# Mixture-of-experts stage: where three pieces of side work are issued (joint-list products on GpSimd, one weight quarter, the third expert's factor copies)

## The chip, the cores and the metric

One core of a Trainium2 chip runs the whole program. A core has five engines, each of which takes its instructions strictly in its own order: TensorE (PE, matmuls; PEld its weight loads), VectorE (DVE), ScalarE (ACT), GpSimd (POOL) and SyncE (SP, which only issues DMAs here). The metric is the device time in microseconds (us) of one execution, the median of the runs; lower is better.

## The reference

Three layers follow each other: a retention layer with a decaying state (input for all that follows: x, 3072 tokens of 512), a soft mixture of experts with 8 experts of 4 slots each, and a sparse mixture of 8 experts of which every token uses the two best.

```python
# last layer; x is (3072, 512), w1 (8, 512, 1024), w2 (8, 1024, 512)
noisy_logits = x @ w_gate + log1p(exp(x @ w_noise)) * noise
top2 = two largest of noisy_logits per token
top2_w = softmax over those two
for e in range(8):
    for k in range(2):
        mask = top2[:, k] == e
        h = maximum(x[mask] @ w1[e], 0)
        out[mask] += top2_w[mask, k, None] * (h @ w2[e])
```

The layer before makes x as c @ slot_out with only 32 slots: every row of x is a mixture of the same 32 vectors, with the weights c.

## The kernel before

The last layer uses that form. With x = c @ slot_out, x @ w1[e] is c @ (slot_out @ w1[e]), so an expert's first weight matrix V1[e] is first multiplied with the 32 slot vectors (g_dot) into a small factor; its split into a high and a low part (g_split) is laid out over the partitions as the factor tile gs, for expert 0 by matmuls (g_rep), for the others by 16 SyncE DMAs of 32 KB (g_copy, L741). Experts are numbered from 0 here, so the third one is expert 2.

Every expert's tokens are gathered as blocks: six full ones of 128 tokens and one of 64 (number 6). Which tokens a block holds is computed on the chip as lists. For experts 0 and 1 there is a list each (lists): a comparison on VectorE (bm, L754), two products on GpSimd (bt, L757 and L758), more comparisons (oh, L761), 24 small matmuls (pli, L765), and two VectorE instructions that give the indices. The lists of the other six experts are made together (lists_all), in two rounds that run during expert 0's blocks and expert 1's first ones: VectorE comparisons bm, rk and oh, two GpSimd products sb (L804), two VectorE products bta of bm and sb (L807), 24 matmuls (L812). lists_all is a generator; it is moved on by one step at the end of the blocks in PACED, (expert, block) = (0, 1) to (0, 5) and (1, 0), and its matmuls are issued at HOOK (0, 4, 4) and (1, 1, 2), that is before step 4 of block 4 of expert 0 and step 2 of block 1 of expert 1.

Of a block, GpSimd gathers the rows of c (fetch, L851) by an indirect DMA, ScalarE and VectorE split them (turn, L863 to L865), TensorE transposes them (L870), multiplies them with the factor tile (hidden, L904; evicted by L907 on ScalarE and L909 and L912 on VectorE), and then with the second matrix V2[e] in 24 matmuls (main, L937 to L939; the small block L941 and L943). V2 is used as a high and a low part too: split_hi is a cast on ScalarE (wh, L879), split_lo a subtraction on VectorE (wl, L885). ScalarE writes the block's result yo (L946), and GpSimd scatters it with an addition into the output (add_rows, L918). Blocks are taken in the order 0, 1, 2, 3, 6, 4, 5 in expert 0 and 0, 6, 1, 2, 3, 4, 5 in the others.

Weights of the coming experts are loaded in quarters of 512 KB, which SyncE issues (L958): V2[e + 1] and V1[e + 3]. The instructions' order on each engine is made when the program is built: an instruction can be placed as soon as what it depends on is there, with the order of the code as priority, however far ahead of its place in the code that is. To tie something to a block's end, a one-element copy on ScalarE reads yo and writes into the tile that the later instruction will fill; these copies are called marks (L777 in lists_all, L957 for the weight quarters). V1[2] is an exception: three of its quarters are loaded after routing (L698), and the last one (L995) after a one-element GpSimd copy (L994) that stands behind the fetches of expert 0. After that quarter, g_rest (HOOK (0, 0, 6)) finishes the product of V1[2] and issues the 16 copies of expert 2's factor tile. The fills (L144) are matmuls without a use.

Of the kernel before, what the change touches and what calls it, by code (L numbers as in the profile page):

```python
# [26 lines left out]
KD = DM // P  # L27
# [78 lines left out]
def kernel(ctx: ExitStack, tc: tile.TileContext, q, k, v, phi, w1, w2,  # L106
                              wg, wn, noise, v1, v2, csta, cst, cst16, out):
    nc = tc.nc
# [24 lines left out]
    def after(*ins):  # L133
        stack = ExitStack()
        for i in ins:
            stack.enter_context(tc.issue_after(i.ins if hasattr(i, "ins") else i))
        return stack
# [22 lines left out]
    def col16(name):  # L160
        o, n = CONST_COLS[name]
        return ct16[:, o:o + n]
# [16 lines left out]
    W1, W2, V1, V2 = {}, {}, {}, {}  # L179
# [30 lines left out]
    with ExitStack() as actx:  # L210
# [284 lines left out]
        wsl = late.tile([P, NCH, E], F32, name="wsl")  # L495
# [50 lines left out]
    with rctx, bctx:  # L546
# [146 lines left out]
        V1[2] = ringp.tile([P, 4096], F32, name="w", tag="w")  # L693
        v1p = v1[2].rearrange("(k p) n -> p k n", p=P)
        with after(put):
            nc.scalar.copy(V1[2].rearrange("p (k n) -> p k n", k=KD)[0:1, :KD - 1, 0:1], wsl[0:1, :KD - 1, 0:1])
        for i in range(KD - 1):
            nc.sync.dma_start(V1[2][:, 1024 * i:1024 * i + 1024], v1p[:, i])  # L698


# [15 lines left out]
    def g_split(pg, n):  # L716
        gr = cc.tile([P, 2, n, QF], F32R, name=f"gr{n}", bufs=1)
        pv = pg[:, :n * QF].rearrange("p (n f) -> p n f", n=n)
        nc.scalar.copy(gr[:, 0], pv)
        nc.vector.tensor_tensor(gr[:, 1], pv, gr[:, 0], op=OP.subtract)  # L720
        return gr

    def g_tile(e):
        gs = cc.tile([P, 4, QF], F32R, name="gs", bufs=4)
        GS[e] = gs.rearrange("p h (k f) -> p (h k) f", f=P)
        return gs

    def g_rep(e, gr, n):
        gs = g_tile(e)
        for g in range(4):  # L730
            gw = psC.tile([P, QF], F32, name="gw", tag="phc", bufs=4)
            for i in range(2):
                nc.tensor.matmul(gw, pselr[32 * g:32 * g + 32, i, :], gr[32 * g:32 * g + 32, i, n],
                                 start=(i == 0), stop=(i == 1))
            nc.scalar.copy(gs[:, g], gw)

    def g_copy(e, gr, n):
        gs = g_tile(e)
        for q in range(4):
            for g in range(4):  # L740
                nc.sync.dma_start(gs[32 * q:32 * q + 32, g].bitcast(F32), gr[32 * g:32 * g + 32, q // 2, n].bitcast(F32))  # L741
# [32 lines left out]
    def lists_all():  # L774

        def mark(ap, y):
            nc.scalar.copy(ap, y[0:1, 0:1])  # L777

        rv = rr.rearrange("p (e c) -> p c e", e=E)
        bv = blk.rearrange("p (c e) -> p c e", e=E)  # L780
        y = yield
        bm = cc.tile([P, NCH, E, LB], F16, name="bma", bufs=1)
        mark(bm[0:1, 0, 0, 0:1], y)
        nc.vector.tensor_tensor(bm, bv[:, :, :, None].to_broadcast([P, NCH, E, LB]),
                                col16("iotab")[:, None, None, :LB].to_broadcast([P, NCH, E, LB]), op=OP.is_equal)
        for i in range(2):
            rk = cc.tile([P, NCH, E], F16, name="rk", bufs=1)
            mark(rk[0:1, 0, 0:1], y)
            nc.vector.tensor_tensor(rk, sels[i], rv, op=OP.mult)
            rs = cc.tile([P, NCH], F32, name="rs", bufs=1)  # L790
            nc.vector.reduce_sum(rs, rk, axis=AX.X)
            rh = cc.tile([P, NCH], F16, name="rh", bufs=1)
            nc.vector.tensor_copy(rh, rs)
            y = yield
            oh = cc.tile([P, NCH // 8, P, 8], F16, name="oh", bufs=1)
            for c in range(NCH // 8):
                mark(oh[0:1, c, 0, 0:1], y)
                nc.vector.tensor_tensor(oh[:, c], tab, rh[:, None, 8 * c:8 * c + 8].to_broadcast([P, P, 8]),
                                        op=OP.is_equal)
            y = yield  # L800
            bt = cc.tile([P, NCH, 2, E, LB], F16, name="bta", bufs=1)
            sb = cc.tile([P, 2, NCH, E], F16, name="sb", bufs=1)
            for a, name in enumerate(("base", "tok")):
                nc.gpsimd.tensor_tensor(sb[:, a], sels[i], col16(name)[:, :, None].to_broadcast([P, NCH, E]),  # L804
                                        op=OP.mult)
                mark(bt[0:1, 0, a, 0, 0:1], y)
                nc.vector.tensor_tensor(bt[:, :, a], bm, sb[:, a, :, :, None].to_broadcast([P, NCH, E, LB]), op=OP.mult)  # L807
            yield
            if i == 0:
                pl = psC.tile([P, 2, E, LB], F32, name="pli", tag="pt")  # L810
            for c in range(NCH):
                nc.tensor.matmul(pl.rearrange("p a e b -> p (a e b)"), oh[:, c // 8, :, c % 8],  # L812
                                 bt[:, c].rearrange("p a e b -> p (a e b)"),
                                 start=(i == 0 and c == 0), stop=(i == 1 and c == NCH - 1))
            if i == 0:
                y = yield
        lt = cc.tile([P, E, LB], F32, name="lta", bufs=1)
        nc.vector.tensor_scalar_add(lt, pl[:, 0], float(N))
        ls = cc.tile([P, E, LB], I32, name="lsa", bufs=1)
        nc.vector.tensor_tensor(ls, lt, pl[:, 1], op=OP.add)  # L820
        for e in range(2, E):
            LS[e] = ls[:, e]
        for g in range(G):
            fetch(2, g)
        yield
# [17 lines left out]
    CG, HOOK = {}, {}  # L843

    def fetch(e, g):
        bs = grp(e, g)
        cg = CG[e, g] = cc.tile([P, 3, NS + E], F32, name="cg", bufs=5)
        if SB in bs:
            nc.gpsimd.memset(cg[TL:, 2, :], 0.0)
        for i, b in enumerate(bs):  # L850
            nc.gpsimd.indirect_dma_start(out=cg[:rows(b), i, :], out_offset=None, in_=ctab,  # L851
                                         in_offset=index(e, b, rows(b)))
            WT[e, b] = cg[:rows(b), i, NS + e:NS + e + 1]
# [127 lines left out]
    with after(his[3], *lists(0, cc, psC, LB)):  # L981
        gr0 = g_split(pgs, 2)
        g_rep(0, gr0, 0)
        pg2 = psC.tile([P, QF], F32, name="pg", tag="phc", bufs=4)
        g_dot(2, pg2, range(KD - 1))
        fill(psC, "pyc", FA)
        fetch(0, 0)
        cg0 = CG[0, 0]
        ga = turn(0, 0)
        fill(psC, "pyc", FT)  # L990
        with after(*ga):
            for g in range(1, G):
                fetch(0, g)
            nc.gpsimd.tensor_copy(V1[2][0:1, 3072:3073], cg0[0:1, 0, 0:1])  # L994
            nc.sync.dma_start(V1[2][:, 3072:], v1p[:, 3])  # L995
        for i in range(4):
            if i > 1:
                split_hi(0, i)
            split_lo(0, i)
        h0, relu = hidden(0, 0)  # L1000
        with after(relu[RL]):
            turn(0, 1)
        HOOK[0, TZ[0], TZ[1]] = (turn, 0, G - 1)
        with after(h0, *ga):
            g_copy(1, gr0, 1)
            lists(1, cc, psC, LB)
            gen = lists_all()
            next(gen)
            for b in PACED:
                PACE[b] = gen.send  # L1010
            HOOK[0, 4, 4] = HOOK[1, 1, 2] = next, gen
    def g_rest():
        g_dot(2, pg2, [KD - 1])
        g_copy(2, g_split(pg2, 1), 0)

    HOOK[0, 0, 6] = g_rest,
    for e in range(E):
        pre = {g: [] for g in range(G)}
        if e + 1 < E:
            pre[0] += [(fetch, e + 1, g) for g in range(G)] if e != 1 else []  # L1020
            for g, at_b in enumerate(TURN):
                HOOK[e, at_b[0], at_b[1]] = (turn, e + 1, g, [] if e else LAST)
            if e >= 2:
                pre[0] += [(g_one, e + 1)]
            pre[0] += [(load_paced, V2, v2, e + 1, e, (0, SB, 1, 2) if e else (0, 1, 2, 3))]
            if e + 3 < E:
                pre[0] += [(load_paced, V1, v1, e + 3, e, (3, 3, 4, 4))]
            pre[G - 1] += [(split_w, e + 1)]
        for g in range(G):
            for f, *a in pre[g]:  # L1030
                f(*a)
            if g + 1 < G:
                last, relu = hidden(e, g + 1)
                LAST[:] = last, relu[-1]
            elif e + 1 < E:
                hidden(e + 1, 0)
            main(e, g)
# [81 lines left out]
```

## Time and profile before

| | |
|---|---|
| median of 3 runs | 589.7 us (586.41, 589.7, 592.46) |
| profiled execution | 592.0 us, of which the span is 590.2 us |
| TensorE busy | 554.7 us, 94% of the span |
| VectorE, ScalarE, GpSimd busy | 255.3, 243.7, 222.5 us |
| mean granted TensorE clock | 0.964 |

The span is the time from the first to the last instruction of one execution that the hardware profiler recorded; the profiled time holds the little that lies around it. Busy shares are averages over stages: routing ends near 212 us, expert 0's first block starts near 225 us, and its last block ends near 279 us. The granted clock is the share of TensorE's full speed (2.4 GHz) that it was allowed; 0.50 is its lower level, 1.2 GHz.

### The profile page before, as it was taken

What the parts mean: (1) busy time and instruction counts of PE and PEld (TensorE: products, weight loads), DVE (VectorE), ACT (ScalarE), POOL (GpSimd) and SP (SyncE); (2) the same over time, 40 slices, a digit from 0 to 9 for tenths busy, and PEclk for the clock granted to TensorE, in tenths of its full rate; (3) what the DMA queues carried; (4) which work ended last, traced back from release to release, by engine and by line L of the source; (5) the groups of instructions that cost most, each with busy time, mean ns of one, the idle gap of its engine ahead of it and who ended that gap; (6) DMA issues with size and microseconds to landing.
All of it is one profiled execution on the core that took longest, in us unless ns stands there. A gap on an engine that the chain in (4) does not pass through costs nothing. (4 is left out here: it accounts for less than half of the span.)

```text
span 590.2 us, 10723 instructions
## 1 busy us (share of the span) xinstructions
PE 554.7 (94%) x4196; PEld 421.8 (71%) x4196; DVE 255.3 (43%) x529; ACT 243.7 (41%) x543; POOL 222.5 (38%) x214
## 2 busy tenths in 40 slices
PE   7999999999899878979999999999999999999990
PEld 4787888787443436858787787787787787788880
DVE  3566777764202366456625235235235234334200
ACT  2555656553101235245246246246345335335210
POOL 3524534330103055642455444344344436332231
PEclk7899999999699789989999999999999999999997
DMA  9999999998799942465446646656656644553232
GB/s 218 286 270 306 299 328 281 308 405 364 291 404 389 367 124 67 102 179 151 108 98 182 125 132 186 124 151 168 137 140 170 143 112 65 132 105 46 37 43 31
DMA packets 79485, 111.76 MB, mean 189 GB/s; under 512 B 10066, under 2 KB 51602, under 8 KB 78530
## 3 DMA queue, kind: packets, MB, share of 16 engines
q1 hardware_dynamic: 65808, 95.96, 49.3%
q0 software_dynamic: 9696, 14.37, 16.7%
q10 hardware_dynamic: 3922, 0.66, 0.6%
q8 instruction: 35, 0.57, 0.4%
q14 instruction: 24, 0.20, 0.1%
HBM read 87.92 MB, written 20.41 MB: 184 GB/s over the span
## 5 line engine op out<-in xcount | busy, mean ns | idle before, releaser
L937 PE MATMUL pyc<-wh,hhl 128*128 128x512 f32 x384 | 154.6, 403 | 0.2 <-ACT hhl L907 0.2
L938 PE MATMUL pyc<-wl,hhl 128*128 128x512 f32 x384 | 152.1, 396 | 0.0
L939 PE MATMUL pyc<-wh,hhl 128*128 128x512 f32 x384 | 151.5, 395 | 0.0
L918 POOL DMA_INDIRECT out_dram<-yo,lsa x42 | 66.1, 1575 | 136.1 <-ACT w L957 31.6
L909 DVE SCALAR_TENSOR_TENSOR hhl<-phc,hhl 128x512 fp32r<-128x512 f32 (+1 forms) x128 | 66.9, 551 | 84.9 <-ACT hhl L907 84.5
L939 PEld LDWEIGHTS pyc<-wh,hhl 128*128 128x128 f32 x384 | 72.6, 189 | 16.6
L937 PEld LDWEIGHTS pyc<-wh,hhl 128*128 128x128 f32 x384 | 72.1, 188 | 16.1 <-ACT hhl L907 0.4
L946 ACT ACTIVATE yo<-pyc,cg 128x512 f32<-128x512 f32 x48 | 33.0, 688 | 121.0 <-PE pyc L939 108.1
L938 PEld LDWEIGHTS pyc<-wl,hhl 128*128 128x128 f32 x384 | 72.4, 189 | 14.6
L907 ACT ACTIVATE hhl<-phc 128x512 fp32r<-128x512 f32 (+1 forms) x128 | 59.5, 513 | 8.0 <-PE phc L904 6.6
L885 DVE TENSOR_TENSOR wl<-w,wh 128x1024 fp32r<-128x1024 f32 x32 | 39.1, 1225 | 49.6 <-ACT wh L879 49.6
L851 POOL DMA_INDIRECT cg<-ctab,lsa x42 | 43.8, 1042 | 15.2 <-issue 14.9
L879 ACT CAST wh<-w 128x1024 fp32r<-128x1024 f32 x32 | 33.4, 1047 | 32.3 <-DMA w<-in_moe_w_dram 24.7
L298 DVE TENSOR_TENSOR am<-pa,cta 128x512 f32<-128x512 f32 x48 | 33.1, 692 | 28.6 <-PE py L322 15.3
L918 POOL DMA_INDIRECT out_dram<-yo,ls x14 | 25.0, 1787 | 47.4 <-ACT w L957 16.2
L256 POOL TENSOR_TENSOR comp<-raws,cta 64x512 f32<-64x512 f32 x24 | 24.9, 1039 | 40.7 <-PE py L322 16.5
L276 DVE TENSOR_TENSOR qT<-pt,cta 64x512 f32<-64x512 f32 x48 | 33.0, 688 | 16.6 <-PE pt L271 16.2
L256 POOL TENSOR_TENSOR vl<-raws,cta 64x512 f32<-64x512 f32 x24 | 24.9, 1038 | 33.5 <-PE py L322 22.6
L904 PE MATMUL phc<-cts,gs 128*128 128x256 f32 (+1 forms) x192 | 36.5, 299 | 0.5 <-ACT cts L873 0.5
L904 PEld LDWEIGHTS phc<-cts,gs 128*128 128x128 f32 x192 | 29.8, 191 | 7.3 <-issue 2.5
L294 PE MATMUL pa<-qT,kT 64*128 64x128 f32 x384 | 31.7, 296 | 0.7 <-DVE qT L276 0.7
L294 PEld LDWEIGHTS pa<-qT,kT 64*128 64x128 f32 x384 | 27.0, 198 | 5.2 <-issue 3.7
(195 smaller groups left out, 701.6 us busy)
## 6 DMA issues: line engine op xcount, KB each, us to landing
w<-in_moe_w_dram SPq DMA_DIRECT2D x80, 512.0 KB, 5.1
w<-in_moe_w_dram SPq DMA_DIRECT2D x11, 2048.0 KB, 10.5
comp<-in_q_dram SPq DMA_DIRECT2D x12, 512.0 KB, 6.7
out_dram<-zt SPq DMA_DIRECT2D x6, 1024.0 KB, 9.8
raws<-in_k_dram SPq DMA_DIRECT2D x11, 512.0 KB, 5.6
raws<-in_v_dram SPq DMA_DIRECT2D x11, 512.0 KB, 7.8
gs<-gr SPq DMA_DIRECT2D x112, 32.0 KB, 2.3
w<-in_moe_w_dram SPq DMA_DIRECT2D x2, 1024.0 KB, 21.1
```

The costliest lines, as they stand in the source:

```text
L256: pool_ins[0] = nc.gpsimd.tensor_tensor(VL[j][rs], RAW[u][1][gs, :, r, :], gv[gs, r, t, :, None].to_broadcast([64, H, D]), op=OP.mult)
L294: mm = nc.tensor.matmul(pa[s][:, hp, :], KT[j][r, hp, :], QT[t][r, hp, g, :], start=True, stop=True)
L851: nc.gpsimd.indirect_dma_start(out=cg[:rows(b), i, :], out_offset=None, in_=ctab, in_offset=index(e, b, rows(b)))
L879: ins = nc.scalar.copy(wh, V2[e][:, 1024 * i:1024 * i + 1024])
L885: nc.vector.tensor_tensor(wl, V2[e][:, 1024 * i:1024 * i + 1024], WH[e][i], op=OP.subtract)
L904: nc.tensor.matmul(ph[:, w * i:w * i + w], GS[e][:, kf + i], CT[e, g][:, :w], start=True, stop=True)
L907: relu.append(nc.scalar.activation(h[:, :, :w], pv, AF.Relu))
L909: last = nc.vector.scalar_tensor_tensor(h[:, :, w + t0:w + t0 + 2 * P], pv[:, :, :2 * P], 0.0, h[:, :, :2 * P], op0=OP.max, op1=OP.subtract)
L918: nc.gpsimd.indirect_dma_start(out=out, out_offset=index(e, b, n), in_=y, in_offset=None, bounds_check=N - 1, oob_is_err=False, compute_op ...
L937: nc.tensor.matmul(py, hhl[:, kf, ts], wh, start=(kf == 0), stop=False)
L938: nc.tensor.matmul(py, hhl[:, kf, ts], wl, start=False, stop=False)
L939: nc.tensor.matmul(py, hhl[:, kf, tl], wh, start=False, stop=(kf == KF - 1))
```

## The change

Three edits. In lists_all, a mark on the product tile sb is put ahead of each of the two GpSimd products, so that they wait for the block's result, as the VectorE products behind them did already. The last quarter of V1[2] is loaded by the same loop as the other three, and its own GpSimd copy and load behind the fetches are gone. The copies of expert 2's factor tile are taken out of g_rest, which now keeps only the split, and are issued at HOOK (0, 3, 5), before step 5 of block 3 of expert 0.

```diff
         with after(put):
-            nc.scalar.copy(V1[2].rearrange("p (k n) -> p k n", k=KD)[0:1, :KD - 1, 0:1], wsl[0:1, :KD - 1, 0:1])
-        for i in range(KD - 1):
+            nc.scalar.copy(V1[2].rearrange("p (k n) -> p k n", k=KD)[0:1, :, 0:1], wsl[0:1, :KD, 0:1])
+        for i in range(KD):
             nc.sync.dma_start(V1[2][:, 1024 * i:1024 * i + 1024], v1p[:, i])
...
             for a, name in enumerate(("base", "tok")):
+                mark(sb[0:1, a, 0, 0:1], y)
                 nc.gpsimd.tensor_tensor(sb[:, a], sels[i], col16(name)[:, :, None].to_broadcast([P, NCH, E]),
                                         op=OP.mult)
...
         fetch(0, 0)
-        cg0 = CG[0, 0]
         ga = turn(0, 0)
         fill(psC, "pyc", FT)
         with after(*ga):
             for g in range(1, G):
                 fetch(0, g)
-            nc.gpsimd.tensor_copy(V1[2][0:1, 3072:3073], cg0[0:1, 0, 0:1])
-            nc.sync.dma_start(V1[2][:, 3072:], v1p[:, 3])
...
     def g_rest():
         g_dot(2, pg2, [KD - 1])
-        g_copy(2, g_split(pg2, 1), 0)
-
+        gr2.append(g_split(pg2, 1))
+
+    gr2 = []
     HOOK[0, 0, 6] = g_rest,
+    HOOK[0, 3, 5] = (lambda: g_copy(2, gr2[0], 0)),
```

## Rows read from the trace of the kernel before

**Rows 1.** Busy time by stretch: bounds, length, busy per engine, granted clock, DMA share, GB/s

```profile
211.92:215.37 3.45, 0.00 (x1) 0.14 (x1) 2.65 (x4) 3.45 (x6) 3.29 (x4) 1.00 0.98 351
254.04:257.75 3.71, 0.00 (x0) 0.03 (x1) 3.71 (x8) 1.56 (x9) 2.31 (x1) 1.00 0.46 114
257.82:261.24 3.42, 3.42 (x11) 2.79 (x12) 0.16 (x1) 1.63 (x7) 0.00 (x0) 0.50 0.59 103
262.00:582.00 320.00, 314.91 (x1599) 250.54 (x1597) 119.20 (x246) 133.50 (x300) 130.80 (x103) 1.00 0.54 123
```

**Rows 2.** Timeline, VectorE, GpSimd, TensorE: start, length, instruction, count, idle before and releaser

```profile
211.81 0.33 DVE L754 TENSOR_TENSOR bm<-blk,ct 128x168 f16<-128x168 f16 x1
212.03 1.98 POOL L804 TENSOR_TENSOR sb<-sel,ct 128x192 f16<-128x192 f16 x2 [3.36 <-PE pg L185]
213.98 0.92 POOL L757 TENSOR_TENSOR bt<-bm,ct 128x168 f16<-128x168 f16 x1
214.86 0.47 POOL L758 TENSOR_TENSOR bt<-bm,ct 128x168 f16<-128x168 f16 x1
215.37 1.57 PE L765 MATMUL pli<-bt,oh 128*128 128x14 f16 x24 [3.45 <-POOL bt L758]
```

**Rows 3.** Timeline, GpSimd, first gather of expert 0

```profile
217.63 1.91 POOL L851 DMA_INDIRECT cg<-ctab,ls  x1 [2.31 <-DVE ls L770]
```

**Rows 4.** Timeline, SyncE's queue, 209 to 262 us

```profile
210.51 1.30 SPq L698 DMA_DIRECT2D w<-in_moe_w_dram  x3
215.68 2.53 SPq L741 DMA_DIRECT2D gs<-gr  x3
227.79 0.34 SPq L995 DMA_DIRECT2D w<-in_moe_w_dram  x1
228.18 18.97 SPq L741 DMA_DIRECT2D gs<-gr  x29
247.25 14.96 SPq L958 DMA_DIRECT2D w<-in_moe_w_dram  x5
```

**Rows 5.** Timeline, ScalarE and TensorE, expert 0's blocks 0 to 3

```profile
237.81 0.19 ACT L957 COPY w<-yo 1x1 f32<-1x1 f32 x1
242.19 0.69 ACT L946 ACTIVATE yo<-pyc,cg 128x512 f32<-128x512 f32 x1 [4.18 <-PE pyc L939]
252.43 1.05 ACT L879 CAST wh<-w 128x1024 fp32r<-128x1024 f32 x1 [4.06 <-DMA w<-in_moe_w_dram]
257.75 0.67 PE L870 MATMUL ptc<-identr,st 128*128 128x128 f32 x3 [3.72 <-DVE st L865]
```

**Rows 6.** One line's instructions: the weight quarters of L958, 262 to 330 us

```profile
DMA to landing us min/median/max: 3.4/4.0/6.3
```

**Rows 7.** Timeline, joint lists, first round (block 3 of expert 0)

```profile
261.42 3.02 DVE L807 TENSOR_TENSOR bta<-bma,sb 128x1344 f16<-128x1344 f16 x2
261.60 2.81 POOL L918 DMA_INDIRECT out_dram<-yo,ls  x1 [4.62 <-ACT w L957]
264.66 0.97 POOL L804 TENSOR_TENSOR sb<-sel,ct 128x192 f16<-128x192 f16 x2
268.31 1.68 PE L812 MATMUL pli<-bta,oh 128*128 128x112 f16 x24
```

**Rows 8.** Timeline, joint lists, second round (block 0 of expert 1)

```profile
281.08 1.56 POOL L918 DMA_INDIRECT out_dram<-yo,ls  x1 [4.95 <-ACT hhl L907]
286.25 3.03 DVE L807 TENSOR_TENSOR bta<-bma,sb 128x1344 f16<-128x1344 f16 x2 [2.04 <-ACT bta L777]
290.09 1.68 PE L812 MATMUL pli<-bta,oh 128*128 128x112 f16 x24
```

**Rows 9.** Timeline, TensorE, first matmuls of expert 1's list

```profile
230.34 0.61 PE L765 MATMUL pli<-bt,oh 128*128 128x14 f16 x8 [0.85 <-POOL bt L758]
```

**Rows 10.** Scatters of L918, 236 to 300 us: landing; and the waits of the whole run

```profile
DMA to landing us min/median/max: 2.5/5.4/8.2
...
POOL out_dram L918 <- DMA out_dram<-yo,lsa: 26.7, 10, 5.2
```

## The prediction

> **What bounds the kernel now.** Read the busy time by stretch first [rows 1]: from 262 to 582 us TensorE works 314.91 of 320.00 us at full clock. There a change gains nothing, and a microsecond saved or lost ahead of it moves the end by a microsecond. What can be saved lies where TensorE stands still: the same view has two holes between routing and the second expert, 211.92 to 215.37 and 254.04 to 257.75, and behind the second one 3.42 us at a granted clock of 0.50, that is 1.2 instead of 2.4 GHz, in which TensorE is busy throughout.
>
> Then ask of each hole what ended last. The first ends when GpSimd has the second of the two products of expert 0's list [rows 2]: the list's matmul L765 waited 3.45 us for L758. The products could have begun at 212.14, when VectorE had their operand (L754), but GpSimd was then making two products of the joint lists (L804, 1.98 us), which stand in the code behind expert 0's fourth block. They had no operand that is late, so the build's scheduling placed them there, in front of the products that TensorE waits for.
>
> The second hole ends with VectorE's L865 [rows 5], but VectorE had been held up itself. In the rows of ScalarE the cast L879 of expert 1's first quarter of V2 stands idle 4.06 us for its DMA, and the block results and evictions behind it in ScalarE's order stand with it. Why the quarter came late is read on SyncE's queue [rows 4]: it is issued at 247.25, directly behind 29 copies of the factor tile (18.97 us, 0.65 us each), though the mark that releases it was done at 238.00 (L957, 237.81 and 0.19) [rows 5]. Half of the 32 copies are those of expert 2. And the copies started late because the queue sat behind V1[2]'s last quarter (L995), which was issued at 227.79 after a GpSimd copy that comes behind the fetches.
>
> **Part by part.** The sum is made against the profiled execution: 592.0 us, of which the span is 590.2. It is the slow end of the three runs of before (586.41 to 592.46); their median is 2.3 below it, and I carry the difference over to the median unchanged. One per cent is 5.9 us, as much as these three runs differ among themselves, so it is about what a measurement of this kernel can tell from no change.
>
> 1. *The joint products leave the list of expert 0.* L757 starts when L754 is done, at 212.2 in place of 213.98 [rows 2]. Its length and that of L758 may change, since VectorE's comparisons now run beside both: 1.34 us for the pair as it stands, up to twice 0.92 if both are as slow as L757 was. They end at 213.5 to 214.05 against 215.32, a gain of 1.3 to 1.8; I take 1.4, nearer to the slower end, because the comparisons still run then. All of it lies on the path: list, gather L851 at 217.63 (it waited 2.31 us for the list) [rows 3], then the first block. **Minus 1.4.**
>
> 2. *V1[2]'s fourth quarter with the others.* One more SyncE issue of 0.43 us (1.30 for three) at 211.8, with nothing behind it in that queue until 215.68 [rows 4]. Its 512 KB take 1.5 us more at the 351 GB/s of that stretch [rows 1], so the transfer may still run when the gather, now at 216.2, begins. If the gather had to stand behind all of it, that is 0 to 1.5 us on the path; I take 0, since GpSimd spends 1.91 us on that gather first [rows 3]. Removed are a one-element GpSimd copy (hidden beside gathers) and SyncE's stop from 218.2 to 227.79. The 13 copies of expert 1's tile that now stand behind that stop run on at 218.2 and are done near 227.
>
> 3. *Expert 2's copies later.* The 16 copies (16 x 0.65 = 10.5 us of SyncE) depend on nothing but a split done before block 0 ends, so they may be placed anywhere from there on; but the weight quarters of blocks 0 to 2 now stand ahead of them in the code, and a quarter whose mark is done goes first. So the first quarter of V2[1] is issued at 238.05 in place of 247.25 (behind a few copies, 0.65 each, if they are placed first). Who waits for the copies: expert 2's hidden layer, a whole expert later. Who waits behind them on SyncE: the other quarters of V2[1], whose casts come after expert 0's last block, and V1[3], needed two experts later. Nothing for either.
>
> With the quarter there, the cast L879 doesn't stand idle where it stood, results and evictions run 4 us earlier, and L865 is done before TensorE asks for it: the hole of 3.71 goes, and with it the half clock behind it, which followed on that idle time: 3.42 us of busy work at 0.50 is 1.71 at full clock [rows 1]. **Minus 5.4.** It is 0 if the quarter stays where it was.
>
> What is late next: the same cast. If it is placed in ScalarE's order as soon as its data are expected, it stands ahead of block 1's result, L946 at 242.19 [rows 5]. A quarter lands 4.0 us after issue in the median of the later ones [rows 6], and this one took 5.2 (247.25 to 252.43), with a second quarter right behind it. So landing is between 242.05 and 243.25, the cast takes 1.05, and block 1's result and the evictions behind it come 0.9 to 2.1 us late, or 0 if the cast is placed behind them. One quarter is now alone, so I take a value near the lower end. **Plus 1.2.**
>
> 4. *The joint products held.* ScalarE gets four marks of under 0.2 us each, nothing to it. GpSimd gets a place in line: each product pair now comes behind the block's scatter L918, and VectorE's L807 waits for it. Block 3 first [rows 7]: L807 started at 261.42 and the scatter at 261.60. A scatter alone takes 1.56 us (281.08, [rows 8]), beside L807 it took 2.81. Now 261.60 + 1.56 + 0.3 between instructions + 0.5 (half of L804's 0.97) gives 264.0: L807 comes 2.6 us later and ends near 267.1, against L812's need at 268.31. So the list itself is in time. The evictions of expert 1's hidden layer, if they stay behind L807 in VectorE's order, would be late by up to 2.6; but they are ready sooner than L807 now and will most likely go ahead of it. Between 0 and 2.6 I take 0.
>
> Block 0 of expert 1 is tighter [rows 8]: L807 ran from 286.25 to 289.28, and L812 needs it at 290.09. With the scatter 0.2 behind L807's old start, as in block 3: 286.4 + 1.56 + 0.3 + 0.5 = 288.8, plus 3.03, is 291.8: 1.7 us late if L812 keeps its place among the matmuls, 0 if it is moved back by as much. The nearest row is expert 1's own list, the same sequence of VectorE, GpSimd and TensorE inside running blocks: there TensorE stood 0.85 us [rows 9]. **Plus 0.9.**
>
> One rule speaks against this part. The two L804 took 1.98 us beside VectorE's comparisons and 0.97 without them [rows 2, 7], and the comparisons went on meanwhile: both were slowed, neither seems stopped. The Trainium skill, page "SBUF — State Buffer", section "Who interferes with whom", says that a VectorE instruction with two SBUF inputs and a GpSimd instruction that reads SBUF exclude each other, and that the later one stands until the other is done. By that rule L807 would also wait out the second product, 0.5 more, and the sum would be 4.2 in place of 4.7.
>
> **The sum:** -1.4 - 5.4 + 1.2 + 0.9 = -4.7 us. 592.0 becomes 587.3; on the median, 585.0.
>
> **Rivals.**
> - *No new wait bites.* Cast and L812 are placed behind what would have stood for them. For it: TensorE has other matmuls to take first; against it: both places are within 2 us of their data in the rows. -1.4 - 5.4 = -6.8: 582.9. Chance 0.22.
> - *The holding costs all it can.* VectorE keeps its order and evictions wait 2.6, L812 keeps its place, 1.7: -6.8 + 1.2 + 2.6 + 1.7 = -1.3: 588.4. For it speaks that GpSimd and VectorE take their work strictly in order. Chance 0.15.
> - *The change doesn't do what it says.* Copies wait for nothing late, so the build may place them ahead of the quarter as it placed L804 ahead of the list, and hole two stays: -1.4 + 0.9 = -0.5: 589.2. Chance 0.10.
> - *Slower: held products behind a scatter that must wait for the one before it.* Later in the trace ten scatters stood 26.7 us in all for an earlier one's landing, which comes 2.5 to 8.2 us after issue, 5.4 in the median [rows 10]. The scatter ahead of block (1, 0) is issued at 281.08; from a landing later than 286.4 on, 5.3 us, the products and L812 move with it. At 8.2 they come 2.9 later still: L812 4.6 late, an idle time as long as the ones that the half clock followed, 1.7 more: 6.3. With block 3's 2.6: -1.4 - 5.4 + 1.2 + 2.6 + 6.3 = +3.3: 593.0. Against it: the landing must be at its worst. Chance 0.08.
>
> **How the numbers follow.** The forecast has 0.45. Its own range is 582.5 to 587.5 by the bounds of terms 1 to 4. The range for 8 in 10 takes in the full gain and the costly holding, with the spread of the runs: 581.5 to 590.0. Faster by over 1% is below 583.8: most of the full gain and the lower edge of the forecast, 0.27. Slower by over 1%, above 595.6, needs the last rival and more: 0.04. The rest is 0.69.
>
> **What would show it.** L757 right behind L754, L765 near 214. SyncE issuing a V2[1] quarter about 10 us earlier, before most of expert 2's copies; no hole of 3 us before L870 and no half clock behind it. The cast L879 ahead of or behind block 1's L946 tells the 1.2. L804 directly behind the scatters of blocks (0, 3) and (1, 0), and a TensorE wait before the second L812. It is wrong if that quarter is still issued behind all copies, if hole two has another releaser that is as late, or if L812 stands for several microseconds.

## The result: slower, and the profile after

The changed kernel takes **595.16 us** (588.96 to 599.89, 15 runs) against 589.7 for the kernel before beside it (15 runs); the ratio is 1.0086, with a 95% interval of 1.0056 to 1.0115. A second series of the same kernel gave 592.47 against 591.38, 1.0029 (0.9997 to 1.0061). So the change costs some 1 to 5.5 us; 585.0 was forecast. The profiled execution of the first series took 595.16 us, its span is 593.3. From line 804 of the kernel before on, the changed kernel's lines stand one further down (L805, L808, L813, L919 for L804, L807, L812, L918).

First what was meant to happen. Expert 0's list, timeline of the changed kernel by engine, against [rows 2]:

```profile
205.71 0.32 DVE L754 TENSOR_TENSOR bm<-blk,ct 128x168 f16<-128x168 f16 x1
206.10 0.86 POOL L757 TENSOR_TENSOR bt<-bm,ct 128x168 f16<-128x168 f16 x1 [3.34 <-DVE bm L754]
206.92 0.91 POOL L758 TENSOR_TENSOR bt<-bm,ct 128x168 f16<-128x168 f16 x1
207.88 1.57 PE L765 MATMUL pli<-bt,oh 128*128 128x14 f16 x24 [2.08 <-POOL bt L758]
```

No joint product stands ahead of L757 any more. From L754's start to TensorE's list it is 2.17 us in place of 3.56: 1.4 less.

SyncE's queue, against [rows 4]:

```profile
204.61 1.77 SPq L698 DMA_DIRECT2D w<-in_moe_w_dram  x4
209.57 18.76 SPq L741 DMA_DIRECT2D gs<-gr  x26
236.01 0.39 SPq L959 DMA_DIRECT2D w<-in_moe_w_dram  x1
236.44 3.68 SPq L741 DMA_DIRECT2D gs<-gr  x6
```

The first quarter of V2[1] goes out at 236.01, with no stop ahead of the copies. That is 11.2 us earlier by the trace's clock, but this whole execution runs early; counted from L754 it goes out after 30.3 us in place of 35.4, 5.1 earlier. ScalarE's cast of it is done at 241.6, long before the third block, and TensorE's transposes wait for nothing: hole two [rows 5] is gone. TensorE's timeline of the changed kernel:

```profile
252.14 0.46 PE L871 MATMUL ptc<-identr,st 128*128 128x128 f32 x3
```

Now what was not meant. Timeline of the changed kernel at block (0, 3), by engine:

```profile
255.17 0.19 ACT L777 CAST bta<-yo 1x1 f16<-1x1 f32 x1
...
256.68 1.56 POOL L919 DMA_INDIRECT out_dram<-yo,ls  x1 [3.98 <-ACT hhl L908]
257.68 1.55 POOL L805 TENSOR_TENSOR sb<-sel,ct 128x192 f16<-128x192 f16 x2
...
258.81 3.32 DVE L808 TENSOR_TENSOR bta<-bma,sb 128x1344 f16<-128x1344 f16 x2 [3.21 <-POOL sb L805]
262.05 0.41 DVE L910 SCALAR_TENSOR_TENSOR hhl<-phc,hhl 128x256 fp32r<-128x256 f32 x1
262.39 0.21 DVE L913 SCALAR_TENSOR_TENSOR hhl<-phc,hhl 128x64 fp32r<-128x64 f32 x1
...
262.74 0.60 PE L905 MATMUL phc<-cts,gs 128*128 128x320 f32 x1 [3.17 <-DVE hhl L913]
```

Read it downwards. The marks are done at 255.36. The block's scatter goes first, and starts only 1.3 us later; the products come behind it; VectorE, which has L808 as the next instruction in its order, stands 3.21 us until 258.81. Its two L808 then take 3.32 us, the evictions of the next hidden layer come behind them, and TensorE waits 3.17 us for those. At block (1, 0) the same sequence ends in the list itself:

```profile
286.30 1.56 POOL L919 DMA_INDIRECT out_dram<-yo,ls  x1 [3.80 <-ACT w L958]
287.93 0.97 POOL L805 TENSOR_TENSOR sb<-sel,ct 128x192 f16<-128x192 f16 x2
...
288.47 3.31 DVE L808 TENSOR_TENSOR bta<-bma,sb 128x1344 f16<-128x1344 f16 x2 [5.00 <-POOL sb L805]
...
291.83 1.38 PE L813 MATMUL pli<-bta,oh 128*128 128x112 f16 x18 [2.29 <-DVE bta L808]
```

And each stand is followed by half clock. Busy time by stretch of the changed kernel, columns as in [rows 1] (the two holes, and what follows each):

```profile
259.57:262.74 3.17, 0.00 (x1) 0.03 (x1) 3.17 (x5) 0.00 (x0) 0.00 (x0) 0.89 0.97 280
262.03:268.85 6.82, 6.11 (x32) 5.03 (x33) 4.72 (x18) 2.12 (x6) 0.82 (x1) 0.50 0.14 26
289.54:291.83 2.29, 0.00 (x1) 0.00 (x0) 2.29 (x3) 1.04 (x1) 0.00 (x0) 1.00 0.50 86
292.75:296.16 3.41, 3.41 (x18) 2.92 (x17) 1.61 (x4) 0.19 (x1) 2.68 (x2) 0.50 0.44 150
```

Where the time went is easiest seen from the starts of the block results (L946, after the change L947). The table takes, from each kernel's timeline: the end of expert 0's list (L770) and the start of the first block's main product, both from the start of L754; then the time from that main product to the result of block (0, 3), from there to that of (0, 4), from the result of (1, 0) to that of (1, 1); last the result of block (1, 4), again from L754. What lies ahead of L754 differs from execution to execution (205.7 to 213.8 us) and is left out by this. The names are those of the experiments below.

```
kernel                      list  main   to 0,3  to 0,4  1,0 to 1,1  (1,4)
before                      5.5   13.4   34.8    12.9    10.9        103.9
after                       4.2   17.5   30.8    18.2    14.7        113.1
e9  after, again            4.2   14.8   30.8    18.2    14.9        110.6
e1  hold alone              4.2   13.2   33.9    17.4    13.2        109.5
e2  quarter alone           5.4   13.8   30.4    12.3    10.9         99.2
e3  copies alone            6.0   13.8   32.5    12.3    10.9        101.4
e4  quarter + copies        5.8   14.8   29.3    12.4    10.9         99.2
e5  e4 + first held         4.2   13.8   29.9    17.0    10.9        103.5
e6  e4 + second held        5.9   14.8   29.4    12.3    15.5        103.9
e7  e4 + held early         4.2   14.0   29.7    12.3    10.8         99.3
e8  after, products first   4.2   15.2   28.9    12.8    10.9         99.7
e10 e2 + held early         4.2   15.1   28.6    12.3    10.9         98.8
e11 held early alone        4.2   12.2   33.9    13.8    10.9        102.6
```

The changed kernel gains 4.0 us up to block (0, 3) and loses 5.3 and 3.8 at the two held blocks. In its first profile it also loses 4.1 ahead of the first main product, which is looked at in e9.

### The profile page after: what moved, and what is told of

Same layout as the page of the kernel before. It is cut to its first block, busy times and chain, and to the rows that moved or that the text cites. A ratio compares the mean times of both kernels' runs of the same rounds, so it can differ in the third digit from the quotient of the medians.

```text
span 593.3 us, 10733 instructions
## 1 busy us (share of the span) xinstructions
PE 552.6 (93%) x4196; PEld 421.4 (71%) x4196; DVE 255.4 (43%) x529; ACT 242.9 (41%) x547; POOL 217.1 (37%) x213
## 5 line engine op out<-in xcount | busy, mean ns | idle before, releaser
L939 PE MATMUL pyc<-wl,hhl 128*128 128x512 f32 x384 | 153.8, 401 | 0.0
L919 POOL DMA_INDIRECT out_dram<-yo,lsa x42 | 65.8, 1566 | 132.0 <-ACT yo L947 32.6
L940 PEld LDWEIGHTS pyc<-wh,hhl 128*128 128x128 f32 x384 | 73.5, 191 | 17.1
L938 PEld LDWEIGHTS pyc<-wh,hhl 128*128 128x128 f32 x384 | 73.3, 191 | 15.7
L939 PEld LDWEIGHTS pyc<-wl,hhl 128*128 128x128 f32 x384 | 73.4, 191 | 15.2
L947 ACT ACTIVATE yo<-pyc,cg 128x512 f32<-128x512 f32 x48 | 33.0, 688 | 119.6 <-PE pyc L940 110.6
L852 POOL DMA_INDIRECT cg<-ctab,lsa x42 | 40.9, 974 | 26.4 <-issue 23.5
L905 PE MATMUL phc<-cts,gs 128*128 128x256 f32 (+1 forms) x192 | 37.7, 306 | 8.1 <-DVE hhl L913 3.2
L919 POOL DMA_INDIRECT out_dram<-yo,ls x14 | 24.2, 1725 | 47.3 <-ACT hhl L908 17.5
L905 PEld LDWEIGHTS phc<-cts,gs 128*128 128x128 f32 x192 | 30.4, 196 | 15.6 <-issue 8.8
L294 PE MATMUL pa<-qT,kT 64*128 64x128 f32 x384 | 30.0, 286 | 1.3 <-DVE qT L276 1.3
L294 PEld LDWEIGHTS pa<-qT,kT 64*128 64x128 f32 x384 | 25.2, 188 | 5.8 <-issue 3.7
```

The costliest lines, as they stand in the source:

```text
L294: mm = nc.tensor.matmul(pa[s][:, hp, :], KT[j][r, hp, :], QT[t][r, hp, g, :], start=True, stop=True)
L905: nc.tensor.matmul(ph[:, w * i:w * i + w], GS[e][:, kf + i], CT[e, g][:, :w], start=True, stop=True)
L919: nc.gpsimd.indirect_dma_start(out=out, out_offset=index(e, b, n), in_=y, in_offset=None, bounds_check=N - 1, oob_is_err=False, compute_op ...
L938: nc.tensor.matmul(py, hhl[:, kf, ts], wh, start=(kf == 0), stop=False)
L939: nc.tensor.matmul(py, hhl[:, kf, ts], wl, start=False, stop=False)
L940: nc.tensor.matmul(py, hhl[:, kf, tl], wh, start=False, stop=(kf == KF - 1))
```

## The experiments

My theory after the result was that the holding costs 5 to 8 us and the quarter 3 to 5, and that the copies gain about 4. The first four kernels take the change apart, beside 589.44 us for the kernel before.

**e1, hold alone** (the kernel before with one line more):

```
             for a, name in enumerate(("base", "tok")):
+                mark(sb[0:1, a, 0, 0:1], y)
```

> The kernel before with the marks on the joint products alone. My theory from the two traces: the list of expert 0 ends 1.4 us earlier, but in blocks (0, 3) and (1, 0) the products stand behind the scatter, VectorE waits for them with the evictions behind, and TensorE stands about 3.2 us and 2.3 us, each followed by some half clock worth 1.7 to 2: in all 5 to 8 us more than before. The rival, that the holding costs nearly nothing and the loss is elsewhere, expects 1.4 us less to 1 us more.

597.1 us, ratio 1.0101 (1.0060 to 1.0142). **e2, quarter alone:**

```
...
-        for i in range(KD - 1):
+        for i in range(KD):
             nc.sync.dma_start(V1[2][:, 1024 * i:1024 * i + 1024], v1p[:, i])
...
-            nc.gpsimd.tensor_copy(V1[2][0:1, 3072:3073], cg0[0:1, 0, 0:1])
-            nc.sync.dma_start(V1[2][:, 3072:], v1p[:, 3])
```

> The kernel before with the fourth quarter of V1[2] loaded with the others, alone. My theory: the rest of that product and its split on ScalarE are now placed ahead of the first evictions of expert 0, and the first block starts about 4 us later: 3 to 5 us more than before, with a TensorE hole and half clock between 216 and 228 us. The rival, that those stops in the trace of after were an accident of one execution, expects no change, 1 us less to 1 us more. Both expect the hole before L870 near 254 us to stay, since the 32 copies still stand ahead of the first quarter of V2[1].

584.08 us, ratio 0.9887 (0.9852 to 0.9923); one of its six runs took 2969.87 us and is not in the ratio. **e3, copies alone:**

```
-        g_copy(2, g_split(pg2, 1), 0)
+        gr2.append(g_split(pg2, 1))
...
+    HOOK[0, 3, 5] = (lambda: g_copy(2, gr2[0], 0)),
```

> The kernel before with expert 2's copies issued later, alone. My theory: the first quarter of V2[1] is issued some 10 us earlier, the hole before L870 and its half clock go (-5.4 us), and the cast that is now ahead of block 1's result costs 0.7 to 1.4: about 4 us less than before, 3 to 5. The rival, that the wait only moves to the cast ahead of block 1's result and what it saves is lost there, expects no change within 1 us.

587.29 us, ratio 0.9955 (0.9929 to 0.9982). **e4, quarter and copies** (the changed kernel without the two marks):

> The changed kernel without the marks on the joint products: quarter and copies together. My theory: +4 from the quarter and -4 from the copies, so as before within 1.5 us. The rival, by which the quarter costs nothing, expects 4 us less than before. If the marks were harmless it would be as slow as the changed kernel, 5 us more.

585.58 us, ratio 0.9917 (0.9884 to 0.9950). So the holding is the part that costs: 7.7 us alone by the medians, 6.0 by the ratio (5.6 up to block (1, 4) in its trace), and 9.6 taken from the whole change, or 6.9 with the second series of the changed kernel. Where I had charged the quarter with the late first block, my theory fell: alone it gains 5.4 us, more than the copies. Both remedies turned out to treat one illness. SyncE's queue with the quarter alone, then with the copies alone:

```profile
208.84 1.77 SPq L698 DMA_DIRECT2D w<-in_moe_w_dram  x4
214.03 21.90 SPq L741 DMA_DIRECT2D gs<-gr  x32
237.06 5.85 SPq L958 DMA_DIRECT2D w<-in_moe_w_dram  x2
```

```profile
225.47 0.34 SPq L995 DMA_DIRECT2D w<-in_moe_w_dram  x1
225.86 12.20 SPq L741 DMA_DIRECT2D gs<-gr  x18
238.16 0.53 SPq L958 DMA_DIRECT2D w<-in_moe_w_dram  x1
238.73 4.97 SPq L741 DMA_DIRECT2D gs<-gr  x8
```

With the quarter alone the 32 copies run from 214.03 without a stop and are done at 235.93, a microsecond before the mark that releases V2[1]'s first quarter: all copies may stay ahead of it. With the copies alone the stop at L995 stays, and the quarter passes 11 of the copies. Either way it goes out earlier, 26.9 and 29.1 us after L754 in place of 35.4, so the two don't add up. The copies alone gain less, because there ScalarE's cast stands ahead of block 1's result and waits 6.60 us for its landing, and TensorE stands behind it. ScalarE's timeline:

```profile
242.25 1.05 ACT L879 CAST wh<-w 128x1024 fp32r<-128x1024 f32 x1 [6.60 <-DMA w<-in_moe_w_dram]
243.21 0.69 ACT L946 ACTIVATE yo<-pyc,cg 128x512 f32<-128x512 f32 x1
```

With the quarter alone the build put the cast behind block 1's result and four evictions, where it waits for nothing.

The next four kernels ask what in the holding costs: the scatter in front of the products, or the hold itself; and whether each round pays alone. The kernel before took 590.02 us beside them. **e5 and e6** are the changed kernel with one round held only:

```
+                if i == 0:
+                    mark(sb[0:1, a, 0, 0:1], y)
```

(in e6 it is i == 1).

> The changed kernel with only the first round's products held (behind block 3 of expert zero); the second round's start as soon as the one buffer of them is free. Base: the changed kernel without any holding, 585.6 us, and the changed kernel, 595.2. Theory (each round pays for itself, the products queue behind the block's scatter on GpSimd, VectorE's large product waits for them with the evictions behind it): expert zero's list keeps its 1.4 us, block (0,3) loses some 5 to 6 with its half clock, block (1,0) nothing: 589 to 591 us. Rival (the two blocks are one loss, the second only inherits a clock or a queue that the first upset): the time of the changed kernel, 594 to 596. Rival (the loss is all at block (1,0)): 584 us.

588.99 us, ratio 0.9977 (0.9951 to 1.0002).

> The changed kernel with only the second round's products held (behind block (1,0)); the first round's go to GpSimd at once, ahead of expert zero's list, so the list's 1.4 us are not gained. Theory: block (0,3) as without holding, block (1,0) loses some 4 us with its half clock: 589 to 590.5 us. Rival (block (1,0) only inherits what block (0,3) upset): 585.6 us. In the order of the queues all engines but GpSimd and the marks stand as in the version without holding, which measured 585.6.

588.53 us, ratio 0.9971 (0.9946 to 0.9996). Each round pays for itself. In e6 VectorE's product of the second round (L809 there) stands 5.65 us, against 2.04 for the block's result alone in the kernel before [rows 8], and TensorE stands 2.95 for it:

```profile
279.79 1.55 POOL L920 DMA_INDIRECT out_dram<-yo,ls  x1 [3.87 <-issue]
281.41 0.97 POOL L806 TENSOR_TENSOR sb<-sel,ct 128x192 f16<-128x192 f16 x2
...
285.31 1.67 PE L814 MATMUL pli<-bta,oh 128*128 128x112 f16 x24 [2.95 <-DVE bta L809]
```

Half clock follows each hole for 3.40 us. Busy time by stretch, e5's hole and what follows it, and then what follows e6's:

```profile
258.58:261.80 3.22, 0.01 (x1) 0.03 (x1) 3.22 (x5) 0.00 (x0) 0.46 (x1) 1.00 0.97 273
263.40:266.80 3.40, 3.40 (x26) 2.68 (x26) 2.31 (x8) 0.89 (x4) 0.81 (x1) 0.50 0.02 5
```

```profile
286.80:290.20 3.40, 3.40 (x11) 2.72 (x10) 1.04 (x3) 0.00 (x0) 3.04 (x2) 0.50 0.49 154
```

Wait plus half of that stretch is 3.22 + 1.7 = 4.9 and 2.95 + 1.7 = 4.65; the table has 4.6 for each (17.0 for e5 against 12.4, 15.5 for e6 against 10.9).

**e7** is the changed kernel with the products made and held one block earlier, behind the one-hot compares (the same lines go out of the next step, behind `bt`):

```
+            sb = cc.tile([P, 2, NCH, E], F16, name="sb", bufs=1)
+            for a, name in enumerate(("base", "tok")):
+                mark(sb[0:1, a, 0, 0:1], y)
+                nc.gpsimd.tensor_tensor(sb[:, a], sels[i], col16(name)[:, :, None].to_broadcast([P, NCH, E]),
+                                        op=OP.mult)
             y = yield
             bt = cc.tile([P, NCH, 2, E, LB], F16, name="bta", bufs=1)
```

> The changed kernel with both rounds' products held one block earlier: behind the results of blocks (0,2) and (0,5), where the one-hot compares start, instead of (0,3) and (1,0). GpSimd then does them some 6 us before VectorE wants them. Theory (the price is that the products come late behind the scatter of the very block that releases VectorE): no wait at either block, the list's 1.4 us stay: 584 to 585 us, at or below the version without holding. Rival (holding costs wherever it is, since GpSimd's queue of scatters and fetches is late throughout): 590 us or more, with VectorE's wait for the products at the same two places. Rival (the list's 1.4 us are worth nothing, as something else ends that stage): 585.6.

**583.52 us**, ratio 0.9899 (0.9855 to 0.9942). **e8** leaves the hold where the change has it and turns GpSimd's order round (HELD is the last product, if the step has made one):

```
+            PACE.pop((e, b), tuple)(*[yo][:(e, b) in PACED])
+            with after(*HELD):
                 add_rows(e, b, yo[:r], r)
-            PACE.pop((e, b), tuple)(*[yo][:(e, b) in PACED])
```

> The changed kernel with GpSimd's order turned round at the two blocks: the two held products go ahead of the block's scatter, which is issued after them; the marks and the hold stay. Theory (the wait is the scatter's: it starts 1.6 us after the marks, when the scatter before it has landed, and takes 1.55 itself): VectorE's large product starts some 1.2 us behind the marks instead of 3.5, few evictions are late, the clock stays up: 586 to 588 us. Rival (the hold itself costs, by the marks and the products' own 0.5 to 1.1 us each ahead of the evictions): 593 to 595. In between, about 590: half and half, or the scatters that now come later hold something else up.

584.98 us, ratio 0.9914 (0.9883 to 0.9944). Its timeline, GpSimd and then VectorE (the scatter is L920 there, VectorE's product L809):

```profile
254.03 0.97 POOL L805 TENSOR_TENSOR sb<-sel,ct 128x192 f16<-128x192 f16 x2 [0.28 <-ACT bta L777]
255.43 2.45 POOL L920 DMA_INDIRECT out_dram<-yo,ls  x1 [0.43 <-issue]
...
254.57 3.32 DVE L809 TENSOR_TENSOR bta<-bma,sb 128x1344 f16<-128x1344 f16 x2 [0.28 <-POOL sb L805]
279.59 3.31 DVE L809 TENSOR_TENSOR bta<-bma,sb 128x1344 f16<-128x1344 f16 x2 [2.64 <-POOL sb L805]
```

At block (0, 3) VectorE's product starts 0.28 us after what kept it busy in place of 3.21, at (1, 0) it stands 2.64 in place of 5.00 (2.04 in the kernel before), and both losses are gone with the hold, the marks and the products' own time left in. The edit turns only GpSimd's order round, so the loss is that of the scatter in front of the products. The early hold is as good and simpler: VectorE's products wait for nothing but the block's result, and TensorE works without a gap in both stretches. VectorE's timeline and busy time by stretch in e7:

```profile
254.59 3.03 DVE L809 TENSOR_TENSOR bta<-bma,sb 128x1344 f16<-128x1344 f16 x2
278.77 3.03 DVE L809 TENSOR_TENSOR bta<-bma,sb 128x1344 f16<-128x1344 f16 x2 [2.07 <-ACT bta L777]
```

```profile
252.00:262.00 10.00, 10.00 (x62) 7.77 (x61) 7.79 (x21) 5.57 (x19) 2.67 (x4) 1.00 0.80 210
276.00:284.00 8.00, 8.00 (x52) 6.14 (x51) 4.89 (x6) 2.42 (x6) 4.17 (x4) 1.00 0.50 104
```

The parts now add to 585.6 + 3.4 (e5) + 2.9 (e6) = 591.9 us for the changed kernel, 3.3 short of 595.16. The last three kernels stood beside 591.38 us for the kernel before. **e9** is the changed kernel again, unaltered.

> The changed kernel once more, unaltered. Its first profile has a stretch that no part explains: from the first block's transposes to its main product it lost some 4 us (the evictions wait for results of TensorE whose records ended 1.7 and 5 us before), while the same queues without the late holding (the version that holds one block earlier) have no such stretch. If it belongs to the kernel: it comes again, 594 to 596 us in the median. If it was an accident of one execution: the stretch is gone, the main product starts some 14 us behind expert zero's first compare instead of 17.5, and the median is the sum of the parts, 585.6 + 3.4 (first round held) + 2.9 (second) = 592 us.

592.47 us. In the first profile, TensorE's timeline at the first block reads:

```profile
215.83 0.33 PE L871 MATMUL ptc<-identr,st 128*128 128x128 f32 x2 [1.30 <-ACT st L865]
216.10 0.63 PE L185 MATMUL pg<-w,sotT 128*32 128x256 f32 x6
218.30 1.65 PE L905 MATMUL phc<-cts,gs 128*128 128x256 f32 x6 [1.57 <-issue]
222.61 0.80 PE L905 MATMUL phc<-cts,gs 128*128 128x256 f32 x2 [2.66 <-DVE gr L720]
```

and in the second:

```profile
226.41 0.37 PE L871 MATMUL ptc<-identr,st 128*128 128x128 f32 x2
226.71 0.63 PE L185 MATMUL pg<-w,sotT 128*32 128x256 f32 x6
227.27 1.51 PE L905 MATMUL phc<-cts,gs 128*128 128x256 f32 x8
```

(This execution has a span of 599.3 us; its L754 starts at 213.81, 8.1 us later than in the first profile.) The stretch is gone, and the main product starts 14.8 us after L754, not 17.5. So the same program runs without it too; how often it comes and what it was, two profiles can't say. The granted clock was 0.50 for 10.24 us in both, from 217.65 in the first and from 215.9 in the second. The two held blocks cost in e9 what they cost in the first profile (18.2 and 14.9). **e10** is e2 with the early hold (the edits of e2 and e7).

> The kernel before with the third V1's last quarter loaded with the others and with the joint products held one block early; the copies of expert three's factors stay where they were. All queues but GpSimd's and the marks stand as in the quarter alone (584.1 us). Theory (the list's 1.4 us come on top, less what the quarter's own landing takes back): 582.5 to 583.5 us, at or a little below the version with the copies moved too (583.5), because the cast of the next expert's weights then stands behind three evictions and makes nobody wait. Rival (the list ends nothing once the quarter's landing does): 584 us.

585.14 us, ratio 0.9895 (0.9842 to 0.9949): by its interval no different from e2 or e7. What the early list is worth beside the quarter is therefore not shown: e7 reaches the result of (1, 4) after 99.3 us and e4 after 99.2, e10 after 98.8 and e2 after 99.2. **e11** is the kernel before with the early hold alone (the edit of e7).

> The kernel before with only the joint products held, one block early; nothing else moved. Theory: the products leave expert zero's list (1.4 us earlier) and no wait appears at blocks (0,3) and (1,0); the hole ahead of the cast of the next expert's weights stays and is timed by SyncE's queue, which hangs on the same list's fetches, so most of the 1.4 us come through: 588 to 589.3 us against 590. Rival (the wait for the last quarter of the third V1 or the late cast ends both stretches, whatever the list does): 590 us. Rival (any holding costs): 593 or more.

592.43 us, ratio 0.9998 (0.9962 to 1.0034). The main product starts 1.2 us earlier and the result of (1, 4) 1.3 earlier than in the kernel before, but the profiled execution gives more than that back at its end: the last scatter starts 5.5 us after the start of the last block result (L948 there), in the kernel before 1.0 after it, and GpSimd stood 5.17 us ahead of it for the landing of the scatter before. In the median nothing is seen. It excludes a cost like that of the late hold; a gain of 1.3 us it can neither show nor exclude.

## Why the prediction was wrong, by its own steps

**Step 1, the list, -1.4.** Right for the list (5.5 to 4.2 in every kernel that holds the first round). But the step carried all of it to the first gather, and that gains 0.8: it starts 5.0 us after L754 in place of 5.8, since it comes 0.85 to 0.87 us after the list's end in all kernels with the early list and 0.28 to 0.29 in the others. No row shows surely what it waits for there. Step 2 took back the rest: see there.

**Step 2, the quarter, 0.** Mis-sized in both directions. Ahead of the first main product it costs: without the quarter the early list brings that product to 12.2 (e11) or 13.2 (e1), with it to 13.8 to 15.2 (e5, e7 to e10), so the two steps together are at +0.4 to +1.8 in place of -1.4. Three things are seen in its place. The first gather, which the step took to lose nothing to the transfer, lands later after its issue (2.9 us in e11 without the quarter, 5.2 in e7 with it). The gather's instruction alone, e11 and then e7:

```profile
DMA to landing us min/median/max: 2.9/2.9/2.9
DMA to landing us min/median/max: 5.2/5.2/5.2
```

The rest of V1[2]'s product and its split now stand ahead of the first block's evictions, since nothing keeps them back. And with the list early TensorE waits for the quarter itself. e7, TensorE:

```profile
218.76 0.62 PE L185 MATMUL pg<-w,sotT 128*32 128x256 f32 x2 [0.97 <-DMA w<-in_moe_w_dram]
```

The late gather is the "0 to 1.5" of the step, of which I took the lower end; the other two were not in it. On SyncE it gains, which I had noted as a fact (the stop is removed, the copies run on) and not priced: that alone closes hole two (e2).

**Step 3, the copies, -5.4 and +1.2.** Right in size. From the first main product to block (0, 3) it is 34.8 before and 29.3 in e4, 5.5 less, and 0.5 more is saved behind it, where there was half clock: -6.0 for a net -4.2. The late cast cost TensorE 0.66 to 0.73 us with quarter and copies, 2.5 with the copies alone, where the quarter was issued 2.5 us after its mark, behind copies that still stood ahead of it. The reason was too narrow: the quarter does it without the copies. That the size came out beside a second remedy that the sum didn't price was luck.

**Step 4, the holding, +0.9: this one failed.** "They are ready sooner than L807 now and will most likely go ahead of it. Between 0 and 2.6 I take 0." They stayed behind it; one pair of them stands ahead of it in the changed kernel, seven behind. Ready is not the question for an engine that takes its work in a fixed order, and [rows 9] was not the same sequence: there TensorE reads GpSimd's products itself, with no VectorE instruction between them and no evictions behind one. The delay was also longer than the 2.6: L808 starts 3.45 us after the marks, because the scatter in front didn't start 0.2 us after them but 1.3. It had to wait for the landing of block (0, 2)'s scatter. The trace of the changed kernel has no landings of these scatters; e6 has them, GpSimd's timeline and the landing of the first of the two:

```profile
249.89 1.78 POOL L920 DMA_INDIRECT out_dram<-yo,ls  x1 [4.07 <-issue]
255.69 2.96 POOL L920 DMA_INDIRECT out_dram<-yo,ls  x1 [4.03 <-ACT hhl L909]
DMA to landing us min/median/max: 5.0/5.0/5.0
```

Block (0, 3)'s result is written at 253.4 there, and its scatter starts 0.8 us after the landing at 254.9. At (1, 0) it is the same: result at 278.0, landing at 279.05, scatter at 279.79. The kernel before could have told me. Its scatter at 261.60 [rows 7] starts 0.8 us after the landing (260.8) of the one before, and block (1, 0)'s, at 286.58, 0.75 after that of the scatter at 281.08 (285.83). So the "0.2 after L807" that I carried from one block to the other was where a landing happened to fall, and the releaser named in the row, a mark on a weight tile, is no operand of that scatter. I had this mechanism as the slower rival, with a chance of 0.08, and placed it at block (1, 0) alone, from a landing of 5.3 us on; [rows 10] says that 5.4 is the median. It struck at both blocks. And the half clock after an idle TensorE, which I booked as a gain in step 3, I left out of the costs of step 4 in all rivals but that one. Block (0, 3) measured 5.3 in the whole change and 4.6 alone, block (1, 0) 3.8 to 4.0 and 4.6 alone, against 0 and 0.9; in e1, without the other two parts, they measured 4.5 and 2.3.

So the sum was -4.7 with 0.9 for the holding; with 9 in its place it is +3.4, which lies between the two series (+5.5 and +1.1). The traces give more, 9.2 and 6.7 at block (1, 4); what lies ahead of L754 differs by up to 8 us between executions, and nothing here says why. Without the holding the forecast would have been -5.6; e7, with a hold that costs nothing, has -6.5 (583.52 against 590.02).

**The rule on the shared ports.** Where the second product overlaps the first L808, the pair of L808 takes 3.31 to 3.32 us; where it doesn't (e7) 3.03. So an overlap of 0.43 us costs 0.3. The Trainium skill, "SBUF — State Buffer", "Who interferes with whom", has the later instruction stand until the other is done, which I had put at 0.5 more; the rows agree in direction, with less than the whole overlap. The price is small against the 3.45.

## What to carry to other kernels

An instruction that is held back "until a block's result" takes its place in its engine's queue behind everything that the same result releases. Before moving it, list what else that result releases on that engine, what that waits for in turn (here a scatter for the landing of the last one), and what is queued behind the consumer; then hold it by an earlier result, so that it is done when it is wanted. And when a change carries two remedies for one wait, price each alone: the one I took for a side effect was the better half.

## What the runs showed of the hardware that I had not expected

GpSimd's scatters into the same output go in a chain here: in e6 one lands at 254.9 and the next starts at 255.69, one is issued at 273.91, lands 5.1 us later, and the next starts at 279.79. A block's scatter can therefore start late by most of a landing though GpSimd is idle; whether the chip asks for this order or only the built program, no run says. A scatter that is issued beside the VectorE pair L807 took 1.56 to 2.96 us: of 18 such scatters in these traces 15 end within 0.03 us of the pair's end (in the kernel before the first runs from 261.60 to 264.41, the pair until 264.44), the other three 1.44 to 1.51 us after it. TensorE at 3.2 us of idle time fell to half clock for 3.40 us in e5 and for 6.82 in the changed kernel; after 2.29 us of it for 3.41; in e3 no half clock followed a wait of 2.45 us. And in one execution the readers of TensorE's results started late: L905 ended its first six at 219.95, and ScalarE's first eviction of them started at 222.00, with a cast ahead of it that started at 221.73, 5.0 us after its operand's last record had ended. The ends of matmuls in a profile are modelled, so either may be what was late. It didn't come again in the one other profile of this kernel, and no run here says why.
